# Block-sparse attention with experts: the sampled rows of v by SyncE in place of gathers

## The chip, the core and the metric

The kernel runs on one core of a Trainium2 chip. Five engines work from queues of their own, in order: TensorE (PE, products, with PEld for its weight loads), VectorE (DVE), ScalarE (ACT), GpSimd (POOL) and SyncE (SP), which here only issues DMAs. Sixteen DMA engines serve them. Where one engine needs what another made, its queue stops at a semaphore until it is there, and with it all that is queued behind. The metric is the device time of one execution, in microseconds.

## The reference

```
scores = q k^T / 8                        # 4 batches, 8 heads, 768 tokens, width 64
mask   = |block_i - block_j| <= 1, or block_i or block_j the first or last of 24 blocks of 32,
         or block_j one of three sampled blocks of block_i
attn   = softmax(where(mask, scores, -1e9));  x = attn v       # 3072 tokens x 512
p      = domain_probs / sum(domain_probs)                      # 4 experts
out    = sum over e of p[:, e] * (relu(x w1[e]) w2[e])         # 512 -> 1024 -> 512
```

The numbers of the sampled blocks are an input, the same for all batches and heads: 24 x 3.

## The kernel before

**Attention.** The 22 inner query blocks of a batch are taken in six groups of four (the last has two), and a group in two units, one for each half of the heads. For each query block there are eight slots of 32 keys: three neighbours, the first block, three sampled blocks, the last block. The keys of a slot are copied within the chip (`copy_k`, on GpSimd and ScalarE, at a block number held in a register). The values come anew from memory: a tile `v` holds a pair of query blocks, 128 partitions x pair x 2 x 512, and row `4k + s` of a partition is row k of slot s. Half 0 holds the neighbours and the first block, half 1 the three sampled blocks and the last block.

**Loading v.** In batch one `load_v0` does it, which the change leaves as it is. In batches two to four (`load_v`, L186) a pair takes three DMAs for the neighbours (`window`, L173) and one for the first block (`first_rows`, L178), all issued by SyncE, and for each of its two query blocks one gather (`gather`, L182) of 128 rows by the list `vidx`, issued by GpSimd, whose instruction DMA_INDIRECT is then on its queue. Sampled rows and last block come with the gather. Three tiles take turns. A batch also loads all its v into two of these turns for the units of its two end blocks (`load_batch`, L102).

**Experts.** The products x w1 and hidden w2 fill the rest, in Strassen-like schemes with each operand split into two parts. L709 is the product with w1 (`product`), L779 the one with w2 for batch one (`second`), L943 the one for the later batches (`second7`). Around them VectorE adds the partial results (L728, L753 to L765, L794, L821, L844 to L854, L953). ScalarE rounds an operand (L598, L634, L866) and GpSimd subtracts to get the rest (L599, L635, L867, and L674, L684, L872, L897, L903). While batch one's experts run, weights are prepared and kept in memory (L577, L647, L680, stores by SyncE); for the later batches SyncE loads them back (`wo`, 256 KB, seven buffers, L613; `w2o`, 512 KB, four buffers, L627), each load as soon as TensorE has freed its buffer.

**Order.** All queues are in the order of the program text. The generator `experts` yields after each product; `drive(until)` runs it to a given point, and the units of the next batch's attention stand between such drives, one unit in about 15 us: parts X and T of older units, half a step of experts, then S of this unit and A (the products with v, L355) of the last. Behind these come the loads for later units: `load_q`, `copy_k`, `load_v`. So attention of batch two lies beside the experts of batch one, batch three beside those of batch two, and batch four beside those of batch three. The experts of batch four run alone.

Of the kernel before, what the change touches and what calls it, by code (L numbers as in the profile page):

```python
# [8 lines left out]
F32 = mybir.dt.float32  # L9
# [8 lines left out]
P = 128  # L18
BLOCK = 32
# [4 lines left out]
def attention_moe_kernel(ctx: ExitStack, tc, qb, kb, vr, sampled, sampled_t, probs, w1, w2, out):  # L24
# [60 lines left out]
    def load_batch(b):  # L85
# [10 lines left out]
        for m in range(0, KT, 4):  # L96
            n = min(4, KT - m)
            if b == 0:
                v = whole[:, m:m + n]
            else:  # L100
                v = pool["v"].tile([P, 2, 2, DM], F32, name="v").rearrange("p a b e -> p (a b) e")
            nc.sync.dma_start(v[:, :n], vr[b * S + P * m:b * S + P * (m + n)]  # L102
                              .rearrange("(k p) e -> p k e", p=P))
            vs += [v[:, i] for i in range(n)]
        keys[b] = k, q, vs

    def blocks(t):
        return range(1 + QG * t, min(1 + QG * (t + 1), NB - 1))
# [76 lines left out]

    def load_v(b, t, cs=range(QG)):  # L186
        js = blocks(t)
        for c in range(min(cs), min(max(cs) + 1, len(js)), 2):
            n = min(2, len(js) - c)
            v = pool["v"].tile([P, 2, 2, DM], F32, name="v")  # L190
            window(v, b, js[c:c + n])
            first_rows(v, b, n)
            for i in range(n):
                gather(v, b, i, js[c + i])
                gathered[b, t][2][c + i] = v[:, i]

# [983 lines left out]
    later["x"] = ctx.enter_context(tc.tile_pool(name="xp2", bufs=1))  # L1180
    pool["v"] = ctx.enter_context(tc.tile_pool(name="v2", bufs=3))
    pool["k"] = ctx.enter_context(tc.tile_pool(name="k2", bufs=1))
# [16 lines left out]
    for b in range(1, B):  # L1199
# [5 lines left out]
        for n in range(N + 1):  # L1205
# [7 lines left out]
            if n > 0:  # L1213
                us[n - 1].T(0)
                us[n - 1].T(1)
            drive(start + (n + 0.5) * per)
            if n < N:
# [3 lines left out]
            if n == 1:  # L1221
                copy_k(b, 0)
                load_v(b, 0, (0, 1))
            t = (n - E0 + 2) // 2
            if n % 2 == 0 and 0 < t < NG:
                load_q(b, t)
                copy_k(b, t, (0,))
            elif n % 2 and 0 < t < NG:
                copy_k(b, t, (1, 2, 3))
                load_v(b, t, (0, 1))  # L1230
            if n % 2 == 0 and 0 < t <= NG:
                load_v(b, t - 1, (2, 3))
        drive(start + (N + 1) * per)
# [55 lines left out]
```

## Time and profile before

| | us |
|---|---|
| median of three runs | 1264.42 |
| lowest and highest | 1261.74 to 1268.55 |
| the profiled execution | 1267.42 |
| its span, first to last instruction | 1265.7 |

TensorE is busy for 1205.0 us of the span. The mean granted clock of TensorE over the span is 0.986. The DMA queue of SyncE takes 71.5% of the sixteen engines' time and moves 302.02 MB; the gathers take 6.1% and move 23.07 MB. In the timeline, an entry's first number is its start, the second its length, and a bracket tells how long the engine stood idle ahead of it and who released it.

### The profile page before, as it was taken

What the parts mean: (1) busy time and instruction counts of PE and PEld (TensorE: products, weight loads), DVE (VectorE), ACT (ScalarE), POOL (GpSimd) and SP (SyncE); (2) the same over time, 40 slices, a digit from 0 to 9 for tenths busy, and PEclk for the clock granted to TensorE, in tenths of its full rate; (3) what the DMA queues carried; (4) which work ended last, traced back from release to release, by engine and by line L of the source; (5) the groups of instructions that cost most, each with busy time, mean ns of one, the idle gap of its engine ahead of it and who ended that gap; (6) DMA issues with size and microseconds to landing.
All of it is one profiled execution on the core that took longest, in us unless ns stands there. A gap on an engine that the chain in (4) does not pass through costs nothing.

```text
span 1265.7 us, 32733 instructions
## 1 busy us (share of the span) xinstructions
PE 1205.0 (95%) x12587; PEld 1105.7 (87%) x12587; DVE 861.9 (68%) x1703; ACT 540.2 (43%) x1259; POOL 838.8 (66%) x788
## 2 busy tenths in 40 slices
PE   7888899999999999999999999999999999999997
PEld 4667788888888889998999989898999999999997
DVE  5675577576765567766676776767676776666667
ACT  3673454656564244444542344344443323222221
POOL 6453888878767475765746775576754777666663
PEclk7899999999999999999999999999999999999999
DMA  8674698889977967888878776788886778887774
GB/s 321 186 249 143 218 330 295 310 297 333 319 250 285 329 210 222 277 291 269 263 220 302 257 259 222 253 260 257 272 257 217 234 246 252 265 270 250 249 247 153
DMA packets 214102, 327.18 MB, mean 258 GB/s; under 512 B 17307, under 2 KB 117244, under 8 KB 213948
## 3 DMA queue, kind: packets, MB, share of 16 engines
q1 hardware_dynamic: 206864, 302.02, 71.5%
q0 software_dynamic: 7040, 23.07, 6.1%
q8 instruction: 100, 1.64, 0.5%
q14 instruction: 54, 0.44, 0.1%
q10 hardware_dynamic: 44, 0.00, 0.0%
HBM read 257.35 MB, written 67.68 MB: 257 GB/s over the span
## 4 chain that ended last, share of the span: by engine, by line
PE 63%; DVE 4%; DMA 3%; issue 1%; ACT 1%; SPq 0%; POOL 0%; DVEq 0%; ACTq 0%; POOLq 0%
PE w L709 16%; PE u L943 15%; PE v L709 12%; PE v L943 11%; PE o L355 2%; DMA wo<-kept 2%; PE tp L342 2%; PE po L779 2%; PE s L321 1%; DVE ha L821 1%; PE s L316 1%; DVE tot L953 1%; PE x L374 0%; DMA kept<-t 0%; PE sw L391 0%
## 5 line engine op out<-in xcount | busy, mean ns | idle before, releaser
L867 POOL TENSOR_TENSOR ho<-ha,ho 128x768 fp32r<-128x768 f32 x165 | 323.8, 1973 | 227.6 <-ACT ho L866 216.2
L709 PE MATMUL w<-xo,wo 128*128 128x384 f32 x1536 | 314.2, 341 | 18.4 <-DVE ha L854 9.7
L709 PEld LDWEIGHTS w<-xo,wo 128*128 128x128 f32 x1536 | 269.3, 189 | 32.3 <-DVE ha L854 12.6
L866 ACT CAST ho<-ha 128x768 fp32r<-128x768 f32 x168 | 139.7, 837 | 260.1 <-DVE ha L821 91.0
L709 PE MATMUL v<-xo,wo 128*128 128x384 f32 x1200 | 243.1, 339 | 7.3 <-DVE hl L728 3.1
L943 PE MATMUL u<-ho,w2o 128*128 128x384 f32 x1128 | 228.7, 339 | 0.4 <-issue 0.4
L709 PEld LDWEIGHTS v<-xo,wo 128*128 128x128 f32 x1200 | 211.5, 189 | 13.9 <-DVE hl L728 3.7
L943 PEld LDWEIGHTS u<-ho,w2o 128*128 128x128 f32 x1128 | 198.0, 189 | 2.6 <-issue 2.0
L943 PE MATMUL v<-ho,w2o 128*128 128x384 f32 x888 | 179.4, 338 | 2.0 <-issue 1.5
L943 PEld LDWEIGHTS v<-ho,w2o 128*128 128x128 f32 x888 | 154.8, 188 | 4.0 <-issue 2.3
L333 ACT ACTIVATE p<-s,mx 128x256 f32<-128x256 f32 (+1 forms) x192 | 123.9, 720 | 79.6 <-DVE mx L332 77.7
L953 DVE TENSOR_TENSOR tot<-v,tot 128x384 f32<-128x384 f32 x184 | 97.6, 550 | 56.3 <-PE v L943 53.8
L821 DVE SCALAR_TENSOR_TENSOR ha<-ha,pb 128x384 f32<-128x384 f32 x126 | 129.6, 1029 | 4.4
L953 DVE TENSOR_TENSOR tot<-u,tot 128x384 f32<-128x384 f32 x180 | 98.9, 552 | 47.3 <-PE u L943 46.7
L779 PE MATMUL po<-w2o,hh 128*128 128x512 f32 x384 | 123.9, 404 | 6.0 <-DVE oacc L794 4.3
L332 DVE CUSTOM_DVE_ANT_1 s<-s,mask 128x256 f32<-128x256 f32 (+1 forms) x192 | 80.4, 438 | 50.6 <-ACT p L333 23.4
L182 POOL DMA_INDIRECT v<-in_vr_dram,vidx x88 | 86.1, 978 | 37.6 <-issue 19.0
L599 POOL TENSOR_TENSOR wo<-r,wo 128x256 fp32r<-128x256 f32 x92 | 74.2, 813 | 48.6 <-ACT wo L598 48.4
L779 PEld LDWEIGHTS po<-w2o,hh 128*128 128x128 f32 x384 | 68.6, 188 | 16.7 <-DVE oacc L794 5.6
L779 PE MATMUL po<-w2o,hl 128*128 128x512 f32 x192 | 75.7, 394 | 0.0
L141 POOL COPY kr<-k 128x128 f32 x176 | 46.0, 293 | 36.3 <-PE s L321 31.5
L355 PEld LDWEIGHTS o<-v,pt 128*32 128x32 f32 x2816 | 48.9, 113 | 19.2 <-issue 15.5
(162 smaller groups left out, 1650.1 us busy)
## 6 DMA issues: line engine op xcount, KB each, us to landing
w2o<-kept SPq DMA_DIRECT2D x168, 512.0 KB
wo<-kept SPq DMA_DIRECT2D x318, 256.0 KB
kept<-wo SPq DMA_DIRECT2D x106, 256.0 KB
v<-in_vr_dram SPq DMA_DIRECT2D x171, 128.0 KB
kept<-w2o SPq DMA_DIRECT2D x32, 512.0 KB
r<-in_w_dram SPq DMA_DIRECT2D x16, 512.0 KB
r<-in_w_dram SPq DMA_DIRECT2D x32, 256.0 KB
kept<-t SPq DMA_DIRECT2D x32, 256.0 KB
```

Source lines behind the costliest of these rows:

```text
L182: nc.gpsimd.indirect_dma_start(out=v[:, i, 1], out_offset=None, in_=vr, element_offset=b * S * DM, in_offset=bass.IndirectOffsetOnAxis(ap= ...
L332: nc.vector.tensor_tensor_reduce(sc, sc, mk, -SCALE, 3.0e38, ALU.add, ALU.min, mx[:n])
L333: nc.scalar.activation(p, sc.rearrange("p (a b) r -> p a b r", b=QG), AF.Exp, bias=mx[:n], scale=-1.0, accum_out=self.sums[:n, m:m + 1])
L355: nc.tensor.matmul(o[cs, m], self.pt[:, 2 * m + k, cs], vs[c][:, k, e], start=k == 0, stop=k == 1)
L599: nc.gpsimd.tensor_sub(o[:, 1], src, f32(o[:, 0]))
L709: nc.tensor.matmul(ps, w[:, wi, t], x[:, xi, t], start=fresh and m == 0, stop=m == 3 * KH - 1, skip_group_check=not fresh)
L779: nc.tensor.matmul(p, a[:, js], w[:, i], start=f == 0 and n == 0, stop=f == FT - 1 and n == 2)
L821: nc.vector.scalar_tensor_tensor(block(g, half), src, 0.0, q, op0=ALU.max, op1=ALU.mult)
L866: nc.scalar.copy(o[:, 0], src)
L867: eng.tensor_sub(o[:, 1], src, f32(o[:, 0]))
L943: nc.tensor.matmul(ps, w[:, j, wi, ds], h[:, hi, j], start=fresh and m == 0, stop=m == 5, skip_group_check=not fresh)
L953: nc.vector.tensor_add(t, ps, t)
```

## The change

In batches two to four the gathers go. For each query block and each of its three sampled blocks SyncE issues a DMA of 32 rows (64 KB) whose address is made from a block number in a register. The numbers of a pair (six) are loaded into registers of SyncE half a unit or more ahead (`load_numbers`, called in the loop over the units), for each pair and batch anew. The three tiles of v are now fixed ones, and the first block's and the last block's rows are written into each of them once per batch, when its first pair comes, by one DMA each; whole-v loads of `load_batch` take turns on the same tiles and mark them as overwritten. Batch one keeps its gathers.

```
-    def load_v(b, t, cs=range(QG)):
-        js = blocks(t)
-        for c in range(min(cs), min(max(cs) + 1, len(js)), 2):
-            n = min(2, len(js) - c)
-            v = pool["v"].tile([P, 2, 2, DM], F32, name="v")
-            window(v, b, js[c:c + n])
-            first_rows(v, b, n)
-            for i in range(n):
-                gather(v, b, i, js[c + i])
-                gathered[b, t][2][c + i] = v[:, i]
+    def load_numbers(t, i):
+        for j in pair(t, i):
+            for r in range(NR):
+                numbers[j, r] = nc.values_load(
+                    sbrow[:1, j * NR + r, :1], engines=(ET.SP,), min_val=0, max_val=NB - 1,
...
+    def next_v():
+        turn = fturn[0]
+        fturn[0] = (turn + 1) % 3
+        if len(fixed) == turn:
+            fixed.append([pool["v"].tile([P, 2, 2, DM], F32, name=f"vs{turn}"), None])
+        return fixed[turn]
+    def load_v(b, t, i):
+        js = pair(t, i)
+        if not js:
+            return
+        entry = next_v()
+        v, of = entry
+        window(v, b, js)
+        if of != b:
+            entry[1] = b
+            first_rows(v, b, 2)
+            nc.sync.dma_start(v[3:P:QG, :2, 1],
+                              vr[b * S + S - BLOCK:b * S + S].unsqueeze(1).broadcast_to([BLOCK, 2, DM]))
+        for n, j in enumerate(js):
+            for r in range(NR):
+                rows = vr[bass.ds(numbers.pop((j, r)) * BLOCK + b * S, BLOCK)]
+                nc.sync.dma_start(v[r:P:QG, n, 1], rows)
+            gathered[b, t][2][2 * i + n] = v[:, n]
...
-    pool["v"] = ctx.enter_context(tc.tile_pool(name="v2", bufs=3))
+    pool["v"] = ctx.enter_context(tc.tile_pool(name="v2", bufs=1))
...
+            t = (n - E0 + 2) // 2
+            if n == 1:
+                load_numbers(0, 0)
+            elif t > 0:
+                load_numbers(t - (n % 2 == 0), 1 - n % 2)
             drive(start + (n + 0.5) * per)
```

SyncE's queue in batch three, at the load of a group's first pair. In the names, wo and w2o are buffers of weights, q the queries, v the tile of a pair; before:

```order
396 L613 DMA wo<-kept_3_1_6_4188 128x512
397 L627 DMA w2o<-kept_2_0_1_3656 128x4x256
398 L113 DMA q<-in_qb_dram 128x512
399 L173 DMA v<-in_vr_dram 32x2x512 x3
400 L178 DMA v<-in_vr_dram 32x2x512
401 L613 DMA wo<-kept_3_1_3_4213 128x512
402 L627 DMA w2o<-kept_2_1_0_3799 128x4x256
```

The same place in the changed kernel, where sbrow holds the block numbers and vs is one of the three fixed tiles; four more pairs of the last two rows and then the wo of row 401 follow:

```order
575 L197 TENSOR_LOAD sbrow x6
576 L646 DMA wo<-kept_3_1_5_4144 128x512
577 L646 DMA wo<-kept_3_1_6_4275 128x512
578 L660 DMA w2o<-kept_2_0_1_3701 128x4x256
579 L115 DMA q<-in_qb_dram 128x512
580 L175 DMA vs_2484<-in_vr_dram 32x2x512 x3
581 L227 ISA
582 L227 DMA vs_2484<-in_vr_dram 32x512
583 L227 ISA
584 L227 DMA vs_2484<-in_vr_dram 32x512
```

Between the same two loads of weights SyncE's queue had q and four DMAs of v; it now has q, nine DMAs of v and six register instructions (ISA), and six loads into registers stand a little ahead.

GpSimd's queue in batch four, where a pair is loaded beside the preparation of hidden values (ho, ha) and of sampled keys (kr); before:

```order
751 L903 TENSOR_TENSOR ha<-ha 128x768
752 L137 COPY kr_2943<-k 128x2x128
753 L141 ISA
754 L141 COPY kr_2943<-k 128x128
755 L141 ISA
756 L141 COPY kr_2943<-k 128x128
757 L182 DMA v<-in_vr_dram,vidx 128x512 x2
758 L867 TENSOR_TENSOR ho<-ha,ho 128x768 x2
```

The same place in the changed kernel:

```order
728 L936 TENSOR_TENSOR ha<-ha 128x768
729 L139 COPY kr_2961<-k 128x2x128
730 L143 ISA
731 L143 COPY kr_2961<-k 128x128
732 L143 ISA
733 L143 COPY kr_2961<-k 128x128
734 L900 TENSOR_TENSOR ho<-ha,ho 128x768 x2
735 L143 ISA
736 L143 COPY kr_3675<-k 128x128
```

The two gathers are gone from between the copies of keys and the subtractions; everything else stands in the old order there, as it does on VectorE and ScalarE.

## Rows read from the trace of the kernel before

**Rows 1.** The page of the profile, its first part: busy time of each engine, share of the span and instructions.

```profile
PE 1205.0 (95%) x12587; PEld 1105.7 (87%) x12587; DVE 861.9 (68%) x1703; ACT 540.2 (43%) x1259; POOL 838.8 (66%) x788
```

**Rows 2.** Busy time in four stretches (us from the span's start): attention of batch two, of batch three, of batch four, and what comes after the last attention. Columns: length, then busy us and number of instructions of each engine, granted TensorE clock as a share of 2.4 GHz, share of the DMA engines, GB/s.

```profile
190.00:420.00 230.00, 221.98 (x2344) 190.54 (x2343) 151.62 (x290) 124.80 (x320) 177.65 (x218) 1.00 0.85 303
425.00:680.00 255.00, 248.42 (x2922) 233.16 (x2922) 174.75 (x370) 110.45 (x259) 157.95 (x137) 0.99 0.80 251
680.00:935.00 255.00, 246.15 (x2745) 233.86 (x2744) 183.96 (x353) 107.78 (x243) 172.83 (x142) 0.99 0.81 263
935.00:1230.00 295.00, 293.83 (x1859) 290.11 (x1858) 203.05 (x337) 88.18 (x143) 194.57 (x100) 1.00 0.77 247
```

**Rows 3.** What TensorE waited for between 190 and 960 us, the one row of a DMA: waiting line, releaser, us in total, times, longest.

```profile
PE w L709 <- DMA wo<-kept: 0.7, 1, 0.7
```

**Rows 4.** Timeline of TensorE, the seven entries ahead of which it stood still and GpSimd came from two gathers. Columns: start, us, engine, line, operation, tiles and shapes, count; in brackets the idle time before it and its releaser.

```profile
194.48 0.73 PE L779 MATMUL po<-w2o,hh 128*128 128x512 f32 x2 [1.56 <-DVE oacc L794]
...
264.17 0.73 PE L779 MATMUL po<-w2o,hh 128*128 128x512 f32 x2 [0.85 <-DVE oacc L794]
...
268.74 1.31 PE L709 MATMUL w<-xo,wo 128*128 128x384 f32 x6 [0.44 <-DVE z L765]
...
347.68 0.73 PE L779 MATMUL po<-w2o,hh 128*128 128x512 f32 x2 [1.25 <-DVE oacc L794]
...
352.24 1.31 PE L709 MATMUL w<-xo,wo 128*128 128x384 f32 x6 [0.44 <-DVE z L765]
...
796.77 2.06 PE L709 MATMUL w<-xo,wo 128*128 128x384 f32 x6 [2.60 <-DVE ha L854]
...
877.27 1.31 PE L709 MATMUL w<-xo,wo 128*128 128x384 f32 x6 [3.09 <-DVE ha L854]
```

**Rows 5.** Timeline of GpSimd (POOL) and VectorE (DVE) around the stop that ends at 796.77.

```profile
789.47 0.99 POOL L182 DMA_INDIRECT v<-in_vr_dram,vidx  x1 [0.16 <-issue]
...
790.76 0.95 POOL L182 DMA_INDIRECT v<-in_vr_dram,vidx  x1 [0.30 <-issue]
...
791.35 4.44 DVE L821 SCALAR_TENSOR_TENSOR ha<-ha,pb 128x384 f32<-128x384 f32 x1
791.74 3.62 POOL L867 TENSOR_TENSOR ho<-ha,ho 128x768 fp32r<-128x768 f32 x2
```

**Rows 6.** The same around the stop that ends at 264.17.

```profile
258.85 0.94 POOL L182 DMA_INDIRECT v<-in_vr_dram,vidx  x1 [0.30 <-issue]
...
259.57 3.89 DVE L590 TENSOR_TENSOR r<-r 128x256 f32<-128x256 f32 x1
...
261.89 1.28 POOL L674 TENSOR_TENSOR r<-r,t 128x512 fp32r<-128x512 f32 x1
```

**Rows 7.** Durations (min, median, max in ns) of two lines of VectorE that read two operands from the same memory as GpSimd.

```profile
L590 DVE TENSOR_TENSOR r<-r x14: 424/628/3890, 114.1 to 382.9; 128x256 f32<-128x256 f32 x14
...
L821 DVE SCALAR_TENSOR_TENSOR ha<-ha,pb x126: 557/606/4595, 447.9 to 1239.1; 128x384 f32<-128x384 f32 x126
```

**Rows 8.** The gathers of L182: time from issue to landing, and their summed busy time on GpSimd over the four stretches of rows 2.

```profile
DMA to landing us min/median/max: 3.2/5.2/6.6
...
sum 1035.00, POOL 61.56; mean POOL 15.39
```

**Rows 9.** Durations (min, median, max in ns) of what the queues of SyncE (SPq) and GpSimd (POOLq) issue: rows of a window of v, 32 partitions x 2 x 512; a piece of w1, 128 x 512; and the loading of a block number into a register, with the arithmetic behind it.

```profile
L173 SPq DMA_DIRECT2D v<-in_vr_dram x132: 598/611/2175, 5.2 to 926.8; - x132
...
L613 SPq DMA_DIRECT2D wo<-kept x318: 319/320/1637, 396.4 to 1226.0; - x159
...
L123 POOLq TENSOR_LOAD <-sbrow x44: 287/293/509, 7.7 to 69.3; - x44
L123 POOLq FUSED_REGOPS  x44: 152/152/181, 8.2 to 69.7; - x44
```

**Rows 10.** What SyncE's queue waited for in batch two (the first five rows) and in batches three and four (the last three).

```profile
SPq L577 <- POOL wo L599: 18.3, 17, 3.1
SPq L563 <- POOL wo L599: 15.4, 8, 2.1
SPq L680 <- POOL r L674: 14.6, 13, 2.2
SPq L647 <- POOL w2o L635: 14.2, 6, 3.7
SPq L680 <- ACT t L673: 13.3, 9, 2.7
...
SPq L613 <- PE w L709: 94.0, 82, 5.3
SPq L613 <- PE v L709: 76.1, 55, 3.5
SPq L627 <- PE u L943: 35.2, 37, 5.3
```

**Rows 11.** Timeline of the second pair of a group of batch three: the last of its four DMAs on SyncE, its second gather on GpSimd, and the first product on TensorE that reads it.

```profile
602.13 0.60 SPq L178 DMA_DIRECT2D v<-in_vr_dram  x1
...
608.22 0.95 POOL L182 DMA_INDIRECT v<-in_vr_dram,vidx  x1 [0.30 <-issue]
...
614.98 1.10 PE L355 MATMUL o<-v,pt 128*32 128x64 f32 x64
```

**Rows 12.** Semaphore instructions on TensorE's queue ahead of the products with v.

```profile
L355 PEldq EVENT_SEMAPHORE  x77: 51/51/51, 38.7 to 955.7; - x77
```

More of the change, by code (lines that the diff above doesn't have):

```diff
@@ L100, in load_batch @@
             else:
-                v = pool["v"].tile([P, 2, 2, DM], F32, name="v").rearrange("p a b e -> p (a b) e")
+                entry = next_v()
+                entry[1] = None
+                v = entry[0].rearrange("p a b e -> p (a b) e")
             nc.sync.dma_start(v[:, :n], vr[b * S + P * m:b * S + P * (m + n)]
@@ L184, in gather, with pair @@
             in_offset=bass.IndirectOffsetOnAxis(ap=vidx[:, j:j + 1], axis=0))
-    def load_v(b, t, cs=range(QG)):
-        js = blocks(t)
-        for c in range(min(cs), min(max(cs) + 1, len(js)), 2):
-            n = min(2, len(js) - c)
-            v = pool["v"].tile([P, 2, 2, DM], F32, name="v")
-            window(v, b, js[c:c + n])
-            first_rows(v, b, n)
-            for i in range(n):
-                gather(v, b, i, js[c + i])
-                gathered[b, t][2][c + i] = v[:, i]
+    numbers = {}
+    def pair(t, i):
+        return blocks(t)[2 * i:2 * i + 2] if t < NG else ()
+    def load_numbers(t, i):
[3 more added lines that the diff above has]
+                    sbrow[:1, j * NR + r, :1], engines=(ET.SP,), min_val=0, max_val=NB - 1,
+                    skip_runtime_bounds_check_because="they are numbers of key blocks")
+    fixed = []
+    fturn = [0]
+    def next_v():
[8 more added lines that the diff above has]
+            return
+        entry = next_v()
+        v, of = entry
[10 more added lines that the diff above has]
+            gathered[b, t][2][2 * i + n] = v[:, n]
     one = const.tile([1, 1], F32, name="one")
@@ L1222, in attention_moe_kernel @@
                 copy_k(b, 0)
-                load_v(b, 0, (0, 1))
+                load_v(b, 0, 0)
             t = (n - E0 + 2) // 2
@@ L1229, in attention_moe_kernel @@
                 copy_k(b, t, (1, 2, 3))
-                load_v(b, t, (0, 1))
+                load_v(b, t, 0)
             if n % 2 == 0 and 0 < t <= NG:
-                load_v(b, t - 1, (2, 3))
+                load_v(b, t - 1, 1)
         drive(start + (N + 1) * per)
```

## The prediction

> **What bounds the kernel now.** I read the page first. TensorE is busy for 95% of the span, GpSimd for 66% [rows 1]; so TensorE sets the end, and another engine counts only where it makes TensorE stop. Then I cut the span into stretches. The change touches attention of batches two to four alone, which lies between 190 and 935 us. There TensorE's idle time is 230 - 221.98 = 8.0 us, 255 - 248.42 = 6.6 us and 255 - 246.15 = 8.9 us [rows 2], 23.5 us in all. Nothing that the change takes away can give back more than that. After 935 us, where nothing changes, TensorE idles for 1.2 us in 295. The granted clock stays at 0.99 to 1.00 of 2.4 GHz in all four stretches, so the clock is no term of the sum.
>
> Next, who makes TensorE stop. Of DMAs there is one row with 0.7 us [rows 3]: neither weights nor v are late today. The longer stops wait for VectorE, which has enough time on the whole (151 to 184 us busy per stretch, rows 2) but is late at single places. The timeline tells why. At 791.35 a VectorE instruction that takes 0.557 us at least [rows 7] takes 4.44 us; it ends where two subtractions of GpSimd, run back to back, end (791.74 + 3.62 = 795.36), and these come straight after two gathers [rows 5]. TensorE then stands for 2.60 us until 796.77 [rows 4]. At 259.57 an addition with a shortest time of 0.424 us [rows 7] takes 3.89 us, until GpSimd, again just come from a gather (258.85 + 0.94), ends a series of subtractions at 261.89 + 1.28 = 263.17 [rows 6]. So two gathers hold GpSimd up, work piles up behind them, GpSimd does it without a gap, and VectorE, whose operands lie in the memory that GpSimd reads, cannot get in.
>
> The Trainium skill (SBUF — State Buffer, section "SBUF: two separate sides") says that VectorE with two operands in SBUF and GpSimd lock a port pair for one whole instruction against each other. Rows 5 go further: L821 waited through two instructions of GpSimd, not through the one that was running. By the rule as it stands a pile-up would cost VectorE one instruction, at most, and a good half of what I count below would not be owed to it; the sum goes by the rows.
>
> **What the change removes.** 66 gathers, two per pair. GpSimd's queue is held by a pair of them from 789.47 to 790.76 + 0.95 = 791.71, for 2.24 us [rows 5]; 33 pairs make 74 us, of which 61.6 us show as busy [rows 8]. GpSimd does not set the end, so this is not 74 us of gain. It is worth what TensorE loses by it: the seven stops of rows 4, each after a pair of gathers and a pile-up, 1.56 + 0.85 + 0.44 + 1.25 + 0.44 + 2.60 + 3.09 = 10.2 us. Bounds: nothing, if the pile-ups form without gathers as well (below nothing, if GpSimd, now elsewhere in time, meets VectorE at worse places), and 23.5 us, all idle time. I take four fifths, 8.2 us: in rows 5, with GpSimd free 2.24 us earlier, the first subtraction would be over before or soon after L821 starts, and the two would not run back to back; in rows 6 the series would shift by 2.24 us and still overlap the addition for some of it.
>
> As VectorE and GpSimd meet everywhere, shifted work makes new stops too. The 23.5 us contain 13.3 us that I do not put down to gathers. For new ones I charge 1 us (bounds 0 and 10.2, as much as goes).
>
> DMA traffic: a pair moved three windows and a first block of 128 KB each and two gathers of 256 KB, 1024 KB. It now moves three windows and six times 64 KB, 768 KB, and 18 loads of 128 KB for end blocks come on top: 33 x 256 KB less 2.3 MB, about 6 MB less. The DMA engines are at 0.80 to 0.85 [rows 2] and TensorE does not wait for them: nothing.
>
> **What it adds: SyncE.** Per pair before: 4 x 0.611 = 2.4 us of issuing [rows 9]. After: three windows, 1.8 us; end blocks, 18 x 0.611 / 33 = 0.3 us; six loads into registers; six row loads with a register instruction each. No row has a SyncE DMA with an address from a register. From below: 0.32 us (L613, like the row load a plain list of 2 KB rows) and nothing for the arithmetic, with 0.293 us per register load: 1.8 + 0.3 + 1.8 + 1.9 = 5.8 us, 3.4 us more per pair. From above: 0.611 us (L173, the window with its gaps) and 0.152 us of arithmetic for each, 0.445 us per register load: 1.8 + 0.3 + 2.7 + 4.6 = 9.4 us, 7.0 us more. An outlier of L173, 2.175 us for each row load, would make 18 us. I take the lower end plus the arithmetic, about 4.3 us more per pair, as 32 rows of 2 KB to partitions are nearest to L613.
>
> Does that reach TensorE? Behind these DMAs stand the loads of wo and w2o. In batches three and four SyncE's queue waits for TensorE to free buffers for 94.0 + 76.1 + 35.2 = 205 us [rows 10], so it runs ahead, and 22 x 4.3 = 95 us (154 us at the upper end) fit into the waits. A load that is late by 4 to 7 us has six more buffers of wo ahead of it, each used for about 1 us of product with as much of others between, some 12 us. In batch two the waits are for GpSimd and ScalarE, five rows of 75.8 us in all [rows 10], and 11 x 4.3 = 47 us (77 at the upper end) just fit. I charge nothing; if the cover goes, it costs what the second rival says.
>
> Does v come in time? The second pair of a group is the tight one. Its gather is issued until 608.22 + 0.95 = 609.17 and lands, by the median of 5.2 us [rows 8], at 614.4, while the product that reads it starts at 614.98 [rows 11]. After the change the row loads start at 602.1, where the first block's load stood, and six at 0.37 to 0.76 us are issued by 604.3 to 606.7; with even the gathers' longest 6.6 us they land by 613.3. So v comes earlier than before, and the tight margin grows: nothing. The same wait for a free tile stands ahead of the windows as before.
>
> The Trainium skill (DMA: Bandwidth & Descriptors, section "Latency and other measured facts") gives a floor of about 600 ns for a tensor load, which speaks against this change; the trace has 287 ns as the shortest of 44 [rows 9], so here it does not hold for GpSimd. By that figure a pair would take an estimated 1.8 us more of SyncE's queue than I count.
>
> **What it adds: TensorE's queue.** The products with v wait for nine to eleven DMAs per pair on shared semaphores instead of six, and every wait beyond an instruction's first is a semaphore instruction of 51 ns on its queue [rows 12]. By the order of the changed kernel there are 62 more of them: 3.2 us if all are seen, nothing if they run under the product before. I take 0.5 us.
>
> **Sum.** -8.2 + 1.0 + 0.5 = -6.7 us. The profiled execution took 1267.42 us for a span of 1265.7 us: 1260.7 us for such an execution. It lies 3.0 us above the median of the runs shown, so I forecast 1257.7 us as the median, 0.5% less than 1264.42. Its own range is 1252 to 1261.
>
> **Rivals.** First, the gathers are gone and little comes of it: VectorE and GpSimd go on meeting wherever both have work (the median of L821 is 0.606 us and its longest 4.595, rows 7), and new stops eat what is won. For it: 13.3 us of the idle time have no gather ahead. Against it: the two longest stops of all have one. Taking three tenths of 10.2 us and charging 2 us, -1 us: 1263.
>
> Second, slower: SyncE falls behind in batch two. Stores of finished weights (L577, L647, L680) and loads of raw ones stand behind the row loads; when they are late, buffers come free late, ScalarE and GpSimd cannot make the next weights, and TensorE waits for wo. It decides from the point where the additional issuing per pair exceeds 75.8 / 11 = 6.9 us, which is at (6.9 + 2.4 - 1.8 - 0.3 - 1.8) / 6 = 0.9 us for a row load with its arithmetic. At 1.2 us there the excess is 1.8 us a pair, 20 us in batch two; with the gain of 6.7 us, +13 us: 1278. At 1.05 us it is 10 us, and the result 1268. For it: no row shows such a DMA, and L173 has single ones of 2.175 us. Against it: 0.9 us is three times L613.
>
> Third, more is won: GpSimd, freed of 74 us, and the earlier v also remove stops that I counted as not theirs, half of 13.3 us. Then -13 us: 1251.
>
> **Chances.** Forecast 0.42, first rival 0.30, second 0.18, third 0.10. A measurement of this kernel cannot tell less than 0.5%, 6.3 us, from no change; faster means under 1258.1, slower over 1270.7. Half of the forecast's cases and a little more, all of the third and 0.04 of the first are faster: 0.24 + 0.10 + 0.04 = 0.38. Slower are 0.16 of the second and 0.04 of the first, where new stops outweigh the old: 0.20. The rest, 0.42, is the same. The range, 1248 to 1274, takes in the third rival and the nearer half of the second.
>
> **What would show it.** Right: no DMA_INDIRECT on GpSimd after batch one, its busy time in the three stretches down by some 60 us; L821 without times above 4 us in 190 to 935; TensorE's idle time there down from 23.5 to about 16 us; SyncE's waits for TensorE down but still there; row loads at 0.3 to 0.7 us each. Wrong: rows "PE <- DMA wo" or "DMA v" of more than a microsecond, or "ACT wo <- DMA kept" in batch two (second rival); VectorE's long instructions as many as before at other places (first rival).

## The result: slower by 0.55%

| | us |
|---|---|
| changed kernel, median of six runs | 1271.9 (1270.17 to 1274.53) |
| kernel before, median of six runs | 1265.3 (1261.74 to 1268.55) |
| ratio, with its 95% interval | 1.0055 [1.0036, 1.0074] |
| the profiled execution, and its span | 1274.53, 1272.4 |

The forecast was 1257.7 us, faster. The time is inside the wide range (1248 to 1274), but on the other side of the kernel before.

The first part of the page, after, beside [rows 1]:

```profile
PE 1214.4 (95%) x12587; PEld 1115.1 (88%) x12587; DVE 845.3 (66%) x1703; ACT 540.5 (42%) x1259; POOL 773.3 (61%) x722
```

GpSimd is freed as the change meant: 838.8 us become 773.3. TensorE executes as many products as before and shows 9.4 us more of busy time for them. Products don't grow, so a lower clock is to be looked for. The four stretches, with the columns of [rows 2]:

```profile
190.00:420.00 230.00, 214.89 (x2295) 186.36 (x2294) 135.97 (x284) 120.75 (x312) 150.46 (x190) 0.96 0.79 273
425.00:680.00 255.00, 248.08 (x2869) 231.26 (x2868) 171.80 (x358) 111.48 (x260) 137.96 (x117) 0.99 0.76 249
680.00:935.00 255.00, 251.42 (x2807) 238.87 (x2806) 181.72 (x359) 108.50 (x240) 155.46 (x122) 1.00 0.78 255
935.00:1230.00 295.00, 293.82 (x1860) 290.07 (x1859) 203.10 (x341) 87.94 (x147) 190.97 (x101) 1.00 0.79 252
```

TensorE's idle time was 8.0, 6.6 and 8.9 us in batches two, three and four; it is now 15.1, 6.9 and 3.6. Batch four won what was hoped for, batch two lost it and more, and its granted clock is 0.96 in place of 1.00. The same split shows in one start: the first load of wo from memory, where batch two's share of the work ends on SyncE's queue, starts at 408.2 us and not at 396.4, 11.8 us later; from there to the end of the span it is 864.2 us in place of 869.3, 5.1 us less. 11.8 - 5.1 = 6.7 us, the difference of the spans.

```profile
L646 SPq DMA_DIRECT2D wo<-kept x318: 319/320/1945, 408.2 to 1232.7; - x159
```

The start for the kernel before stands in [rows 9]. A single start is a rough measure: two runs below with almost the same program, e7 and e10, have 397.0 and 389.7 us on one chip. Two questions follow: what batch two loses, and why.

What TensorE waited for between 190 and 960 us (waiting line, releaser, us in total, times, longest):

```profile
PE w L742 <- DVE z L798: 14.4, 2, 7.7
PE w L742 <- DVE ha L887: 2.8, 3, 1.7
...
PE v L976 <- DMA w2o<-kept: 1.4, 1, 1.4
```

Two waits make 14.4 us; before, that line (L709 <- L765) had four of 1.0 us at most. The stops behind ha, 9.4 us before (L854, which is L887 now), are down to 2.8. The first of the two long stops, in the timeline, in order of time:

```profile
216.95 0.41 ACT L631 CAST wo<-r 128x256 fp32r<-128x256 f32 x1 [3.23 <-DVE r L625]
224.19 0.62 ACT L706 CAST t<-r 128x512 fp32r<-128x512 f32 x1 [6.83 <-DMA kept<-t]
224.71 0.52 ACT L760 ACTIVATE hh<-u 128x384 fp32r<-128x384 f32 x1
225.26 1.30 DVE L761 SCALAR_TENSOR_TENSOR hl<-u,hh 128x384 fp32r<-128x384 f32 x1 [7.92 <-ACT hh L760]
...
229.88 0.55 DVE L798 TENSOR_TENSOR z<-w,z 128x384 f32<-128x384 f32 x1
230.48 2.29 PE L742 MATMUL w<-xo,wo 128*128 128x384 f32 x6 [7.74 <-DVE z L798]
```

Read it from the end. TensorE waits for z, made by VectorE. VectorE had waited 7.92 us for hh, made by ScalarE; and ScalarE stood 6.83 us in front of a rounding into t, which is no work that TensorE needs. It stood there because the tile t has two buffers and the store to memory of the one it wants to overwrite (`kept<-t`) had not landed. hh stands behind that rounding in ScalarE's queue. So a late store by SyncE stops TensorE through three engines. The second stop has the same chain behind it: ScalarE stands for 6.17 us, until 315.47, for a store of t issued at 309.56, and TensorE for 6.63 us. The first store is on SyncE's queue (SPq) here:

```profile
201.03 0.65 SPq L680 DMA_DIRECT2D kept<-w2o  x1
205.19 1.30 SPq L610 DMA_DIRECT2D kept<-wo  x3
...
212.38 3.92 SPq L227 DMA_DIRECT2D vs<-in_vr_dram  x6
...
217.04 0.36 SPq L596 DMA_DIRECT2D r<-in_w_dram  x1
217.44 0.46 SPq L713 DMA_DIRECT2D kept<-t  x1
```

The six row loads take 3.92 us, and the store of t comes behind them at 217.44; before it was issued at 212.09:

```profile
212.09 0.43 SPq L680 DMA_DIRECT2D kept<-t  x1
```

Earlier in the changed kernel, between 201.03 + 0.65 = 201.68 and 205.19, SyncE issues nothing for 3.51 us: there stand six loads of block numbers into registers, which this view doesn't list. At two other pairs the same hole is 2.75 us (256.81 to 259.56) and 3.55 us (294.51 to 298.06). Over the eleven pairs of batch two six loads hold the queue for 2.2 to 3.5 us, 2.8 us on the mean or 0.47 us for each load; in batches three and four it is 1.95 us, 0.33 us for each. The median over all 198 loads (min, median, max in ns; first row) hides this. The next two rows are those of batch two and of the later batches apart:

```profile
L197 SPq TENSOR_LOAD <-sbrow x198: 263/273/967, 133.7 to 932.1; - x198
...
L197 SPq TENSOR_LOAD <-sbrow x66: 264/275/967, 133.7 to 352.0; - x66
...
L197 SPq TENSOR_LOAD <-sbrow x132: 263/272/292, 464.4 to 932.1; - x132
...
L227 SPq FUSED_REGOPS  x198: 55/55/65, 143.0 to 942.5; - x198
L227 SPq MOVE vs<-in_vr_dram x198: 29/29/38, 143.1 to 942.6; - x198
L227 SPq DMA_DIRECT2D vs<-in_vr_dram x198: 472/473/1312, 143.2 to 942.7; - x198
```

Of the 66 loads of batch two 22 take 0.4 to 0.97 us, each time some of the first five of a group of six; of the later ones none does. Why, no run shows.

Of SyncE's five waits in batch two that made 75.8 us [rows 10] four leave 18.3 us, and the fifth (L563, now L596, for GpSimd's wo) is under the 0.8 us of the smallest row listed:

```profile
SPq L610 <- POOL wo L632: 9.6, 9, 2.8
SPq L713 <- POOL r L707: 4.2, 4, 1.1
...
SPq L680 <- POOL w2o L668: 2.4, 1, 2.4
...
SPq L713 <- ACT t L706: 2.1, 2, 1.6
```

The other side of the same account is the time in which SyncE's queue is occupied, counted from the end of one of its instructions to the end of the next, without the waits. Of the 195 us from 190 to 385 that is 114 us before and 174 us after. Of the 60 us more the register loads make 25; the larger part is the row loads with their arithmetic, 0.70 us from one to the next.

The clock, in stretches of 2 us around the first stop (length, then busy time and instructions of PE, PEld, DVE, ACT and POOL, clock, DMA share, GB/s):

```profile
222.00:224.00 2.00, 0.74 (x4) 0.26 (x2) 0.00 (x0) 0.00 (x0) 0.00 (x0) 1.00 0.91 344
224.00:226.00 2.00, 0.00 (x0) 0.00 (x0) 0.73 (x1) 1.04 (x2) 1.11 (x1) 0.71 0.76 285
226.00:228.00 2.00, 0.00 (x0) 0.00 (x0) 1.68 (x6) 1.01 (x4) 0.69 (x2) 0.50 1.04 381
...
232.00:234.00 2.00, 2.00 (x7) 1.71 (x6) 0.94 (x2) 0.78 (x2) 2.00 (x2) 0.50 0.34 91
234.00:236.00 2.00, 2.00 (x13) 1.97 (x12) 0.00 (x0) 0.30 (x1) 0.90 (x2) 0.73 0.77 294
236.00:238.00 2.00, 2.00 (x15) 1.77 (x14) 0.00 (x0) 1.95 (x5) 0.73 (x1) 1.00 1.01 376
```

During the stop the clock falls from 2.4 to 1.2 GHz and stays there until about 235: the six products of L742 behind the stop take 2.29 us, where 1.31 was usual [rows 4]. What is lost by it after this stop is about half of 1.52 + 2.0 us and a quarter of 2.0, 2.3 us; after the second (6.63 us, product again 2.29 us) about 2.6 by the same count. With 15.1 - 8.0 = 7.1 us of idle time that is 12.0 us, about the 11.8 us of batch two. That the two agree so closely is partly chance, as starts differ by some microseconds between executions.

### The profile page after: what moved, and what is told of

Read it like the earlier page. It is cut to its first block, busy times and chain, and to the rows that moved or that the text cites. A ratio compares the mean times of both kernels' runs of the same rounds, so it can differ in the third digit from the quotient of the medians.

```text
span 1272.4 us, 33381 instructions
## 1 busy us (share of the span) xinstructions
PE 1214.4 (95%) x12587; PEld 1115.1 (88%) x12587; DVE 845.3 (66%) x1703; ACT 540.5 (42%) x1259; POOL 773.3 (61%) x722
## 4 chain that ended last, share of the span: by engine, by line
PE 64%; DVE 4%; DMA 3%; issue 1%; ACT 1%; POOL 1%; SPq 0%; DVEq 0%; ACTq 0%; POOLq 0%
PE w L742 16%; PE u L976 14%; PE v L742 12%; PE v L976 11%; PE po L812 3%; PE o L388 2%; PE tp L375 2%; DMA wo<-kept 2%; PE s L354 1%; PE s L349 1%; DVE ha L854 1%; DVE tot L986 1%; DVE xo L519 1%; POOL ho L900 1%; ACT p L366 1%
## 5 line engine op out<-in xcount | busy, mean ns | idle before, releaser
L742 PE MATMUL w<-xo,wo 128*128 128x384 f32 x1536 | 317.3, 343 | 21.8 <-DVE z L798 14.4
L742 PEld LDWEIGHTS w<-xo,wo 128*128 128x128 f32 x1536 | 272.7, 191 | 34.3 <-DVE z L798 16.0
L742 PE MATMUL v<-xo,wo 128*128 128x384 f32 x1200 | 245.7, 342 | 3.6 <-DVE hl L761 1.8
L742 PEld LDWEIGHTS v<-xo,wo 128*128 128x128 f32 x1200 | 214.6, 191 | 9.5 <-DVE hl L761 2.1
L854 DVE SCALAR_TENSOR_TENSOR ha<-ha,pb 128x384 f32<-128x384 f32 x126 | 121.8, 967 | 4.4
L632 POOL TENSOR_TENSOR wo<-r,wo 128x256 fp32r<-128x256 f32 x92 | 74.4, 814 | 58.9 <-ACT wo L631 56.9
L631 ACT CAST wo<-r 128x256 fp32r<-128x256 f32 x92 | 37.0, 404 | 49.1 <-issue 13.8
L905 POOL TENSOR_TENSOR ha<-ha 128x768 f32<-128x768 f32 x24 | 51.6, 2151 | 4.6 <-DMA w2o<-kept 2.9
```

The source lines that it names most:

```text
L632: nc.gpsimd.tensor_sub(o[:, 1], src, f32(o[:, 0]))
L742: nc.tensor.matmul(ps, w[:, wi, t], x[:, xi, t], start=fresh and m == 0, stop=m == 3 * KH - 1, skip_group_check=not fresh)
L854: nc.vector.scalar_tensor_tensor(block(g, half), src, 0.0, q, op0=ALU.max, op1=ALU.mult)
L905: nc.gpsimd.tensor_sub(s3, a11, a21)
```

## The experiments

The theory (A): in batch two SyncE's queue has no room; what overfills it, on top of the row loads, are the loads of block numbers into registers. Rivals: one store of t in a wrong place; the row loads themselves; addresses from registers; the loss lies in all batches alike. Ratios are against runs of the kernel before on the same chip, whose median was 1258.71 us in the first group of runs (e1, e2, e3, e6), 1265.72 in the second (e5, e7 to e15) and 1259.74 in the third (e16 to e18). A 0.5% difference between chips is thus normal, and starts in the trace are compared across groups only roughly.

### Which batches: gathers in batch two (e1), rows in batch two alone (e2)

```
+        if b in (1,):                      # e2: if b in (2, 3)
+            window(v, b, js)
+            first_rows(v, b, 2)
+            for n, j in enumerate(js):
+                gather(v, b, n, j)
...
-            elif t > 0:
+            elif t > 0 and b not in (1,):  # e2: not in (2, 3)
```

> Batch two keeps its gathers and loads its first block for each pair, on the fixed tiles; batches three and four load sampled rows by SyncE as changed. Theory S (late stores): the loss lies in batch two, where SyncE's row loads put the stores of t ahead of ScalarE's next cast by some 5 us late, and TensorE stops twice (7.7 and 6.6 us); without them the two stops ahead of 'w' released by 'DVE z' are under 1.5 us each, the first load of wo comes at 395 to 399 us as before, and the gain of the later batches stays: 1257 to 1263 us. Rival P (GpSimd and VectorE meet at worse places without gathers): the time stays above 1265, as batches three and four still go without gathers.

> Only batch two loads sampled rows by SyncE; batches three and four keep gathers, on the fixed tiles. Theory S: both long stops of batch two are there, 6 to 8 us each, with a granted clock of 0.95 to 0.97 in 190 to 420 us, and the first load of wo comes at 406 to 410 us; nothing is won later: 1273 to 1280 us. If the loss were spread over the three batches (rival: DMA traffic of small loads) it would be about a third, 1267 to 1269 us.

Measured: e1 0.9959 [0.9946, 0.9972], e2 1.0061 [1.0039, 1.0082]. With the change in batches three and four the kernel gets faster, with it in batch two alone as slow as with all of it. In e2 the wait for z is there (11.2 us, two), in e1 it is 2.6 us in four. The place of the loss is batch two, at least in the main.

### Is it the one store? Stores of t earlier (e3), by ScalarE (e5)

```
-                        nc.sync.dma_start(k[:, m], t)
+                        (nc.sync if m else nc.scalar).dma_start(k[:, m], t)   # e5
...
+                    if step in (6, 8):                                        # e3
+                        store((step - 6) // 2, 0)
```

> The changed kernel with the two stores of t (L713) moved two steps of the weights' preparation ahead on SyncE, directly behind the cast that fills t; nothing else. Theory S: ScalarE finds t stored in time or nearly so, 'ACT t <- DMA kept<-t' falls from 19 us to under 5, the two stops fall to under 2 us each, the clock in 190 to 420 us is 1.00, and the time is 1256 to 1262 us. Rival T (transfers: the landing takes long because small loads crowd the DMA engines, whenever it is issued): the stores land as late as before and the time stays at 1268 or more. Rival P: no change, 1270 to 1273.

> The changed kernel with the 32 stores of t (L713, the first of each two) issued by ScalarE, behind its own cast, in place of SyncE. Theory S, now wider (SyncE's queue as a whole is too full in batch two: with the stores of t moved ahead the two long stops went, but the stores of wo came late in their stead): SyncE is rid of 32 x 0.39 = 12 us and the stores of t no longer wait behind row loads, so the two stops of 7.7 and 6.6 us go, ScalarE waits less for stores of wo than in the e3 run (22 us), and the ratio to before is 0.996 to 1.003. Rival T (landing is what takes long): stops of 5 us and more stay, ratio 1.005 or more.

Measured: e3 1.0057 [1.0027, 1.0086], e5 1.0040 [1.0017, 1.0064]. In e3 the stop itself is gone, 1.0 us behind z, and the clock in batch two is 1.00; the time didn't move. What ScalarE and TensorE wait for there instead, between 190 and 425 us:

```profile
ACT wo L631 <- DMA kept<-wo: 22.1, 10, 4.2
...
ACT w2o L667 <- DMA kept<-w2o: 7.8, 2, 4.5
```

```profile
PE o L388 <- DMA vs<-in_vr_dram: 5.7, 5, 1.9
```

Now the stores of wo and w2o are the late ones, and v. In e5 the two stops shrink to 8.6 us in all and ScalarE waits for stores of wo. Both runs are slower than expected. The single store was where the lack of room showed, not its cause: moved forward, it pushes others back. Rival T, a landing that takes longer, can be judged by the traces: the store of t at 217.44 frees its buffer after 6.75 us, and in the kernel before, with its gathers, one took 6.63 us (410.10 to 416.73):

```profile
410.10 0.32 SPq L680 DMA_DIRECT2D kept<-t  x1
...
416.73 0.62 ACT L673 CAST t<-r 128x512 fp32r<-128x512 f32 x1 [5.27 <-DMA kept<-t]
```

The landing was as long before; the issue is what came later.

### What fills the queue: no rows after the first (e6), fixed numbers (e7, e10), one register (e11), a gathered control (e8)

```
-                rows = vr[bass.ds(numbers.pop((j, r)) * BLOCK + b * S, BLOCK)]
+                rows = vr[b * S + (7 * j + 5 * r) % NB * BLOCK:...]         # e7, e10
+                rows = vr[bass.ds(numbers[0, 0] * BLOCK + b * S, BLOCK)]    # e11
...
-                load_numbers(0, 0)
+                pass                                                        # e6, e7, e8
```

In e6 the row loads stand behind `if of != b` as the end blocks do, and go to blocks 0 to 2: sampled rows of later pairs are left out. e8 keeps the gathers (`gather(v, b, n, j)` in place of the row loads) and takes over only the fixed tiles with their first block loaded once.

> Sampled rows are loaded only when a tile is first used in a batch, at fixed addresses, and block numbers are not loaded into registers: most pairs are computed with other rows of v. So neither gathers nor row loads. It shows what the gathers cost at most. Theory S: no stop over 2 us in batch two, 1253 to 1260 us, below the e1 run by what batch two's gathers cost, 1 to 5 us. Rival P: GpSimd's work is as in the changed kernel, so the stops of 7.7 and 6.6 us are there too and the time is 1268 or more.

> The six row loads of each pair are issued at fixed addresses, so neither loads into registers (6 x 0.27 us) nor register arithmetic and moves (6 x 0.084 us) are on SyncE's queue: about 2.1 of 7.2 us less per pair. The rows are those of other blocks than the sampled ones. Theory S: as SyncE's queue in batch two is what costs, the loss shrinks by more than a quarter: ratio 0.997 to 1.003. Rival T: bytes and DMAs are the same, ratio 1.005 or more.

> Gathers as before in all batches; of the change only the fixed tiles and the first block's rows once per tile and batch: 24 DMAs of 0.6 us less on SyncE. Theory S: SyncE's queue in batch two is a little emptier, 5 us of 235; within 0.3% of before, rather faster: ratio 0.996 to 1.001. If the fixed tiles cost something themselves (waits of another kind), it is over 1.002.

> The changed kernel with all 198 register loads of block numbers left in place, but each row load goes to a fixed block, so its address is not built from a register (the reading of the right blocks is left out; the same count and size of transfers). Theory A, the register loads are what fills SyncE's queue in batch two (six of them hold it about 3.2 us a pair by the gaps between neighbours in the changed kernel's trace): the time stays with the changed kernel's, 1.002 to 1.008 of before, the first load of wo back from DRAM stays near 408 us, and the stops of TensorE behind z stay above 8 us in sum. Theory B, transfers with an address from a register are what is dear: it goes to where the run with fixed numbers went, 0.988 to 0.995, with the first load of wo near 397 us.

> The changed kernel with one register load in all; every row load takes its address from that one register by the same arithmetic (all rows are read from one block of the batch; the reading of the other numbers is left out). Theory A (register loads): 0.988 to 0.996 of before, near the run with fixed numbers, at most 3 us above it for the 198 address computations of some 0.08 us, which are 1 us a batch-two step; the first load of wo near 397 to 400 us. Theory B (register addresses): 1.002 to 1.008 and stops behind z above 8 us in sum.

Measured: e6 0.9901 [0.9881, 0.9920], e7 0.9911 [0.9877, 0.9945], e8 1.0015 [0.9994, 1.0036], e10 0.9946 [0.9929, 0.9964], e11 0.9933 [0.9907, 0.9960].

e8 says that the tiles are worth nothing: with the gathers the old stop stays, `PE w L738 <- DVE ha L883: 8.1, 4, 3.1`. e7 takes away the register loads and the computed addresses, with all 198 row loads still issued, and the kernel is 0.9% faster than before. e10 was to put the register loads back. Its trace has no row of a TENSOR_LOAD on SyncE: loads whose values nothing reads didn't get into the program, and 198 semaphore instructions of 17 ns stand in their place. It is therefore almost a second run of e7, and the two intervals overlap from 0.9929 to 0.9945; for theory B its number says nothing. e11 does what e10 was to do from the other side: all 198 addresses are computed from a register, but it is loaded once. It is as fast as the fixed ones. So computed addresses cost nothing that can be seen: at a fixed address, in e7, the issue itself takes longer by the median (min, median, max in ns), 0.592 us, than the 0.473 us and 0.084 us of arithmetic above.

```profile
L227 SPq DMA_DIRECT2D vs<-in_vr_dram x198: 468/592/1741, 143.6 to 922.3; - x198
```

The register loads make the difference between 1.0055 and 0.9933. The place in e11 that answers to 201.03 above:

```profile
195.96 0.61 SPq L680 DMA_DIRECT2D kept<-w2o  x1
196.67 2.98 SPq L610 DMA_DIRECT2D kept<-wo  x3
```

The hole between the same two stores is 0.10 us, where it was 3.51. The wait for z is 5.9 us in e11, 4.8 in e7 and 5.3 in e6: some of it comes with fewer loads in the queue too. In e6, whose queue has neither row loads nor register loads for most pairs, ScalarE still stands 3.58 us for a store of t and TensorE 4.51 us behind it. That part of the two stops isn't made by an over-full queue; what makes it was not tested. Three expectations missed by their size: e7 won more than expected, e6 lies 7.6 us under e1 where 1 to 5 were expected, and e8 lies at 1.0015, just outside its 0.996 to 1.001.

### Where a register load costs: numbers kept (e14, e15), loaded early (e16), loaded beside gathers (e17), fixed in batch two (e18)

```
             for r in range(NR):
+                if (j, r) in numbers:
+                    continue
...
-                rows = vr[bass.ds(numbers.pop((j, r)) * BLOCK + b * S, BLOCK)]
+                rows = vr[bass.ds((numbers[j, r] if j < 1 + 2 * 6 else numbers.pop((j, r))) * BLOCK + b * S, BLOCK)]
...
+            if N - 7 <= n < N:                                    # e16, batch one; 7 pairs kept
+                load_numbers((n - N + 7) // 2, (n - N + 7) % 2)
```

e14 and e17 have e1's gathers in batch two as well; e17 loads in batch two the numbers that three and four will use. e18 is the changed kernel with e7's edit for batch two alone.

> Gathers in batch two, rows by SyncE in batches three and four, and there the numbers of the first six pairs are kept in registers from batch three to batch four, so that batch four has 36 register loads fewer. Theory A: batches three and four paid about 4.4 us for 132 register loads (864.2 against 859.8 us from the first load of wo to the end, the changed kernel against fixed numbers), so 36 fewer give about 1 us: 0.993 to 0.996, a little under the 0.9959 of the run with gathers in batch two alone. Rival: the later batches have so much waiting in SyncE's queue that the register loads there cost nothing: 0.995 to 0.998.

> The changed kernel with the numbers of the first six pairs kept in registers from batch two on; batch two itself still loads all 66. Theory A (the loss is made in batch two by its register loads): batch two is as in the changed kernel, first load of wo near 408 us, and the time 1.001 to 1.006 of before. Rival (the loss is spread over the three batches): 72 of 198 loads fewer give back a third of the 18 us between the changed kernel and fixed numbers, 0.998 to 1.001.

> The whole change, but the numbers of the first seven pairs (42 of 66) are loaded into registers in batch one, one pair at each of its last steps, and kept for all three batches, so that batch two has 24 register loads in place of 66 and batches three and four 24 each; batch one gains 42. Theory A (the register loads take SyncE's slack in batch two, about 0.5 us each in the queue): 42 fewer there free some 21 us of its queue, the late stores of t go, the sum behind z falls under 7 us, the first load of wo comes near 396 us, and the time is 0.991 to 0.998 of before. Rival (what counts is the row loads, 66 in batch two whatever their addresses; the run with kept numbers but all loads in batch two stood at 1.0011): 0.999 to 1.003.

> Gathers in batch two and rows by SyncE in three and four, as in the run with kept numbers, with the same 96 register loads in all, but 42 of them stand in batch two beside the gathers (their numbers are kept) and so many fewer in batch three. Theory A (a register load costs only where SyncE's queue has no room): batch two's queue has room with the 66 row loads gone, so nothing is lost there, 0.993 to 0.998, within its interval of the run with kept numbers (0.9964). Rival (a register load hurts wherever it stands in batch two, by holding the stores behind it): 42 of 66 loads give back two thirds of the 10 us between the changed kernel and e1, 1.000 to 1.004, with stops behind z above 6 us.

> The changed kernel with fixed blocks and no register loads in batch two alone (its reading of the block numbers is left out); batches three and four read theirs by registers as in the change. Theory A (the loss is made in batch two): the first load of wo comes near 397 us, 11 us earlier than in the changed kernel, and the time is 0.992 to 0.999. Rival (the 132 register loads of batches three and four cost as much each as those of batch two): two thirds of the loss stay, 1.000 to 1.004.

Measured: e14 0.9964 [0.9949, 0.9979], e15 1.0011 [0.9996, 1.0025], e16 0.9956 [0.9939, 0.9972], e17 0.9942 [0.9920, 0.9964], e18 0.9962 [0.9939, 0.9985].

e16 decides, by its time. It does the whole change, with all rows by SyncE in three batches, and differs from e15 in where 42 of the numbers of batch two are loaded, and in keeping seven pairs and not six (12 loads fewer later). They are loaded in batch one, whose queue has waits of up to 15 us (`SPq L596 <- POOL wo L632: 35.8, 6, 15.3` in the changed kernel up to 190 us). That turns 1.0011 into 0.9956. Its trace shows less of the gain: the profiled execution is the slowest of the twelve (1259.98 us, median 1253.75), its first load of wo starts at 396.0 us, as expected, but 9 us after those of e17 and e18 on the same chip (386.8 and 386.9), and its wait for z is 8.9 us, more than the 7 that were expected. Batch two's queue is still nearly full. e18 gets about the same, 0.9962, by fixed numbers in batch two alone. e17 shows that the loads don't hurt by themselves: 42 of them stand in batch two beside gathers, and nothing is lost; there SyncE still waits for its work:

```profile
SPq L619 <- POOL wo L641: 16.6, 12, 3.3
SPq L722 <- POOL r L716: 15.5, 12, 2.8
SPq L605 <- POOL wo L641: 12.5, 7, 2.1
SPq L689 <- POOL w2o L677: 10.5, 5, 3.2
SPq L722 <- ACT t L715: 9.0, 9, 2.7
```

Those five are 64.1 us, nearly the 75.8 of before.

Among the runs without gathers in batches three and four (e9 left out) the occupied time of SyncE's queue between 190 and 385 us sorts the ratios. With 106 to 164 us of the 195 (e1, e6, e7, e10, e11, e14, e16 to e18; e16 is the 164) they are 0.9901 to 0.9964. With 165 to 174 us (e5, e3, e15, the changed kernel) they are 1.0011 to 1.0057. The border between them is no threshold: e16 and e5 are 1 us apart there, and e5 has handed stores to ScalarE. Row loads alone don't reach that (155 us in e7 and e11), nor do 42 register loads beside gathers (123 us in e17); the two together do.

For e15 and e14 theory A is less sharp. e15 has 72 loads fewer in batches three and four and is 0.0044 below the changed kernel, 5.6 us, between what the two theories gave: the later batches' loads cost something too. Of e14's 36 nothing can be seen against e1. e18, which leaves all 132 of them in place, is 0.0029 above e11, which isn't clear of noise. So of the 15 us between the changed kernel and e11 some belong to the later batches; how many stays open.

e1, e14, e16 and e17 read all the right rows and beat both kernels; their intervals overlap, so which of them is best isn't settled.

### An over-full queue (e9)

```
                 nc.sync.dma_start(v[r:P:QG, n, 1], rows)
+                nc.sync.dma_start(v[r:P:QG, n, 1], rows)
```

on top of e1, in batches three and four.

> As the e1 run (gathers in batch two), but in batches three and four each row load is issued twice: 12 in place of 6 per pair, some 3.3 us of SyncE's queue and 0.4 MB more. Theory S: SyncE waits for TensorE there and has room: against the e1 run 0 to 4 us, ratio to before 0.996 to 0.999. If row loads cost in these batches as they do in batch two, 22 pairs at 1 us a pair: ratio 1.010 or more.

Measured: 1.2364 [1.2331, 1.2397], 300 us more. This wasn't the dose that was meant. The second load of the same rows waits on SyncE's queue for the landing of the first, and everything behind waits with it; the largest wait of SyncE's queue, and TensorE's largest:

```profile
SPq L235 <- DMA vs<-in_vr_dram: 233.3, 132, 4.8
```

```profile
PE o L396 <- DMA vs<-in_vr_dram: 125.7, 20, 9.1
```

132 waits of 1.77 us. It says what a blocked queue costs, nothing on the price of a row load.

## Why the prediction was wrong

**"Just fit. I charge nothing" is the step that failed.** The prediction compared the additional issuing in batch two, 11 x 4.3 = 47 us, with SyncE's waits there, 75.8 us, and charged nothing because the first was smaller. With the true sizes (next paragraph) it is 73 us, which would still just fit, and batch two lost 11.8 us. So sum against sum was the wrong test: waits add up over 230 us, but a store that is due within a few microseconds can't use a wait that comes later. In the changed kernel waits are still 20 of the 195 us from 190 to 385, and stores of t are late all the same. Even with 2.8 us less per pair (e7, e10, e11, without the register loads) some wait for z remains, 3.5 to 5.9 us; part of it, as e6 shows, is there without a full queue.

**SyncE's term was too small as well.** The prediction took "the lower end plus the arithmetic, about 4.3 us more per pair". By the trace of the changed kernel a pair of batch two holds the queue, gaps included, for 2.2 us with its windows, 0.3 with its share of end blocks, 2.8 with the register loads and 4.2 with the row loads: 9.5 us, 6.6 more than the 2.9 us that the four DMAs of before take by the same count. That is near the upper bound (7.0), not the value taken. A row load was put near L613's 0.32 us, 0.47 with its arithmetic, and takes 0.70; L173, the window with its gaps, was the nearer row. A register load was put at its busy time, 0.293 us, and holds the queue in batch two for 0.47, more than the upper bound of 0.445; the 44 loads read for it stood in another part of the kernel and on another queue.

**The rule that was set aside.** The prediction read the Trainium skill (DMA: Bandwidth & Descriptors, section "Latency and other measured facts"), with its floor of about 600 ns for a tensor load, as refuted by a shortest row of 287 ns. The changed kernel agrees with the prediction: the shortest of 198 loads is 263 ns, and a load holds the queue for 0.33 us in the later batches and 0.47 us in batch two. Only single loads of batch two take 0.6 us and more.

**The second rival was the mechanism**, with 0.18. Stores late, buffers free late, ScalarE stops: all of that came. But its price didn't: its threshold of 6.9 us per pair lies just over the measured 6.6, so by its own rule it would have cost nothing. It also expected the wait at wo. What "PE <- DMA wo" was to show didn't come (0.8 us); the sign was the wait for z and "ACT <- DMA kept" in front of t.

**"The clock is no term of the sum" failed** by some 5 us, which the two stops of 7 us cost behind them. It wasn't quite true of the kernel before either: the product behind the stop of 2.60 us takes 2.06 us where 1.31 is usual [rows 4], and from 796.8 to 800.4 us the granted clock is 0.54. The mean of a stretch hid it:

```profile
796.80:800.40 3.60, 3.60 (x12) 3.60 (x13) 2.00 (x4) 0.00 (x0) 0.00 (x0) 0.54 0.10 38
```

**What was right, and what was luck.** The gathers' term, -6.7 us with new collisions and semaphores: the eight runs in which batch two's queue has room (e1, e7, e10, e11, e14, e16 to e18) lie at 0.9911 to 0.9964, and 0.9947 was forecast. That the cause was the gathers' pile-ups is supported by e8, which keeps gathers and keeps the stops, and by two lines of VectorE in the changed kernel: L854, which was L821 before with up to 4.595 us, and L623, which was L590 with up to 3.890 us [rows 7]:

```profile
L854 DVE SCALAR_TENSOR_TENSOR ha<-ha,pb x126: 557/712/2216, 459.5 to 1245.8; 128x384 f32<-128x384 f32 x126
...
L623 DVE TENSOR_TENSOR r<-r x14: 424/426/853, 116.2 to 394.4; 128x256 f32<-128x256 f32 x14
```

Batch four's idle time fell by 5.3 us, near the 2.60 + 3.09 of its stops [rows 4]. The rest of the agreement is luck. Of the 10.2 us of stops 4.5 lay in batch two, but three of the eight runs (e1, e14, e17) keep batch two's gathers, and without them TensorE idles there for 6.8 us in e7 and 8.7 in e11, against 8.0 before; batch three, where no stop was counted, gained 1.2 and 1.9 us in these runs instead. Batches three and four on SyncE's queue gave room, as said; the wait for v didn't grow. The products with v have 102 semaphore instructions and not 77 [rows 12], 25 more where 62 were expected, 1.3 us if all are seen; what they cost can't be told from these runs.

```profile
L388 PEldq EVENT_SEMAPHORE  x102: 51/51/51, 39.6 to 962.5; - x102
```

## What to carry to other kernels

A queue that only issues transfers is a resource with its own busy time: count each register load and each issue by what it holds of the queue in the stretch where it stands, as a median over the whole kernel can hide the slow ones, and check the room stretch by stretch against what is due within a few microseconds. When a stop's chain ends in a store of something that nobody downstream needs, ask what stood ahead of that store; moving it alone only makes another late. Small values that don't change are best loaded where the queue waits anyway, and kept.

## What the runs showed of the hardware that was not expected

Six register loads hold SyncE's queue for 1.95 us in the later batches and for 2.2 to 3.5 us in batch two, where single ones take up to 0.967 us. The store of t takes 6 to 7 us from issue to the release of its buffer (217.44 to 224.19; 410.10 to 416.73 before), so two buffers give little slack. In the two long stops TensorE's clock went to 1.2 GHz, for some 10 us around the first. Before, it went there behind the stop of 2.60 us (0.54 from 796.8 to 800.4) and not behind that of 3.09 us, whose product took 1.31 us [rows 4]. Writing the same place twice by DMA cost a wait of 1.77 us on the issuing queue each time.
